# Attention in front of a mixture of experts: softmax scaling moved behind the product with v, float32 scores in batch 0

## The chip, the cores and the metric

One core of a Trainium2 chip. The metric is device time in microseconds of one launch. TensorE (PE) multiplies, VectorE (DVE), ScalarE (ACT) and GpSimd (POOL) do elementwise work, and SyncE (SP) issues most DMAs. A matmul takes a stationary operand, which a weight load (PEld) brings in, and streams a moving operand past it into PSUM; ScalarE and VectorE read PSUM, GpSimd works on SBUF only.

## The reference

Three stages in a row, float32 in and out:

1. Attention with 2 batches, 8 heads, 576 positions and 64 columns a head. The score of query i and key j is `q.k/8 - (cum[i] - cum[j])`, where `cum` is the running sum of `max(s, 0)`; keys behind the query are masked. The row is shifted by its maximum, `exp` is taken, and it is divided by its sum plus 1e-9. The result is multiplied with `v`.
2. A mixture of 8 experts over the 1152 tokens (512 wide, 1024 hidden): gates by `exp` of logits and eight rounds of row and column normalisation, then `relu(x @ w1) @ w2` of every expert, weighted and summed.
3. A feed-forward layer of 2048 hidden units with softplus.

## The kernel before, in words

Products are exact enough because each float32 operand is split in a rounded part and a rest (`h` and `l`, type F32R): a product of two split operands is three F32R matmuls, h*h, h*l and l*h. An unsplit F32 matmul is one call in the code; in the trace it is two TensorE instructions.

Attention works on pairs of heads, four pairs in each batch, eight in all (p = 0 to 7). The two heads lie in the two halves of the 128 partitions, so a score matmul uses 64 rows for each head and the two run side by side. A pair has five units (i = 0 to 4): units 0 to 3 are blocks of 128 queries, with 128, 256, 384 and 512 keys; unit 4 is the last 64 queries of both heads together (576 keys, stationary operand `ends`, 128 rows). For a unit the steps are:

- `scores`: q*k as products of split operands (unit 0: one F32 matmul), plus one F32R matmul that adds the bias from the running sums (`bq`, `bk`, `be`).
- `softmax` on VectorE (mask, minimum, negated), `expo` on ScalarE (exp and row sum), `norm`: VectorE takes the reciprocal of the row sum, GpSimd multiplies the unit's exponentials by it.
- `transp` on TensorE, `evac` on ScalarE (PSUM to SBUF), `attend` on TensorE: `v` times the transposed block, F32, one half of the array's columns for each head. Units 0 to 3 collect in one PSUM tile `pv`, unit 4 in `pv4`.
- After unit 3 and after unit 4, ScalarE (`do_X`) and VectorE (`do_Y`) split the result into `xh` and `xl`.

The order of work is written out by hand. A loop over n issues, in the order `YSUKAXVWBTPED`, `scores` of unit n+1 (S), `transp` of unit n-LT (T), `evac` of n-LV (V), `attend` of n-LA (A), `softmax` of n (B), `expo` of n (E), with LN, LT, LV, LA = 2, 3, 4, 5. K splits q and k of the next pair (hi on ScalarE, rest on GpSimd), D copies the last 64 queries into `ends`, W splits the first expert's weights, U (from n = `ready`) runs the first group of the first expert's up product between attention units. Each engine works through its own instructions in order. PSUM tiles rotate: `sc` has 4 buffers (two units), `tr` has 2, `pv` has 1.

At the start the running sums are split into four arrays (`cs`, each also negated), written to DRAM (`c8d`), and read back into single partitions of `bk`, `bq` and `be` (`load_bias`, L245 to L251). All of these DMAs, the loads of q, k, v and the raw weights are issued by SP in program order. After attention the experts and the last layer run as one long stream of matmuls (`up`, L127; `down`, L174).

Of the kernel before, what the change touches and what calls it, by code (L numbers as in the profile page):

```python
# [14 lines left out]
ALU = mybir.AluOpType  # L15
# [5 lines left out]
def attention_moe_ffn(ctx, tc, q, k, v, s, w_gate, w1, w2, w_in, w_out, out):  # L21
# [59 lines left out]
    def prep_steps(e, which, i, parts=1):  # L81

        if e >= NE:
            return
        key = (e, which, i)
        t = raw_t.pop(key)
        hi = w_p.tile([P, WQ], F32R, tag=f"w{which}h", name=f"w{which}h")
        lo = w_p.tile([P, WQ], F32R, tag=f"w{which}l", name=f"w{which}l")
        c = KD if which == 1 else TQ
        wt[key] = (hi.rearrange("p (c n) -> p c n", c=c), lo.rearrange("p (c n) -> p c n", c=c))  # L90
        nc.scalar.activation(out=hi, in_=t, func=AF.Copy)  # L91
        for a in range(parts):
            yield
            r = slice(a * WQ // parts, (a + 1) * WQ // parts)
            (nc.gpsimd if parts > 1 else nc.vector).tensor_tensor(out=lo[:, r], in0=t[:, r], in1=f(hi[:, r]),  # L95
                                                                  op=ALU.subtract)
        load_next()
# [92 lines left out]
    with tc.manual_schedule():  # L190
# [3 lines left out]
        with ExitStack() as att:  # L194
            early = ExitStack()
            eb_p = [(early.enter_context(tc.tile_pool(name="eb", bufs=10)), 10)]
# [23 lines left out]
            def load_rest(p):  # L220
                b, hp = divmod(p, NP)
                if p > 0:
                    load_bias(p)
# [13 lines left out]
            def init_bias(x):  # L237
                for t in (bq_t[x], bk_t[x], be_t[x]):
                    nc.gpsimd.memset(f(t), 0.0)
                for j in range(2):  # L240
                    for t, cols in ((bq_t[x], slice(0, S)), (bk_t[x], slice(0, S)),
                                    (be_t[x], slice(j * REM, (j + 1) * REM))):
                        nc.gpsimd.memset(f(t[j * D:j * D + 4, cols]), 1.0)  # L243

            def load_bias(p):  # L245
                for j in range(2):
                    h = 2 * p + j
                    nc.sync.dma_start(out=f(bk_t[p % BB][j * D + 2:j * D + 4, :]), in_=c8d[h, 0:2, :])
                    nc.sync.dma_start(out=f(bq_t[p % BB][j * D:j * D + 2, :]), in_=c8d[h, 2:4, :])
                    nc.sync.dma_start(out=f(be_t[p % BB][j * D:j * D + 2, j * REM:(j + 1) * REM]),  # L250
                                      in_=c8d[h, 2:4, NB * P:])  # L251
# [3 lines left out]
            for n in range(4):  # L255
                load(n)
# [8 lines left out]
            cs = [eb_tile(B * H, f"cs{x}").bitcast(F32R) for x in range(4)]  # L265
            c8d = dr.tile([B * H, 4, S], F32, name="c8d")
            for a, b in ((0, 2 * P), (2 * P, S)):
                x = c8[:, a:b]
                nc.scalar.activation(out=cs[0][:, a:b], in_=x, func=AF.Copy)
                nc.scalar.activation(out=cs[2][:, a:b], in_=x, func=AF.Copy, scale=-1.0)  # L270
                nc.vector.tensor_tensor(out=cs[1][:, a:b], in0=x, in1=f(cs[0][:, a:b]), op=ALU.subtract)
                nc.vector.tensor_tensor(out=cs[3][:, a:b], in0=f(cs[0][:, a:b]), in1=x, op=ALU.subtract)
            for x in range(4):
                nc.sync.dma_start(out=c8d[:, x, :], in_=f(cs[x]))
            load_bias(0)
            make_identity(nc, ident)
# [15 lines left out]
            for x in ends:  # L292
                for y in x:
                    nc.gpsimd.memset(f(y), 0.0)
# [3 lines left out]
            def split(n, engine=nc.gpsimd):  # L298

                p, r = divmod(n, 2)  # L300
                if p >= B * NP:
# [9 lines left out]
            def split_ends(p):  # L311
# [3 lines left out]
                t = pair[p]  # L315
                t["ends"] = ends[p % 2]
                for y, z in zip(ends[p % 2], (t["qh"], t["ql"])):
                    for j in range(2):
                        r = slice(j * D, (j + 1) * D)
                        o = y[r, j * REM:(j + 1) * REM]  # L320
                        if p > 0:
                            nc.sync.dma_start(out=f(o), in_=f(z[r, W:]))
                        else:
                            nc.vector.tensor_copy(o, f(z[r, W:]))
# [4 lines left out]
            def scores(u):  # L329
# [5 lines left out]
                if i > 0:  # L335
                    kh, kl = t["kh"], t["kl"]
                else:
                    for j, x in enumerate(sc):
                        r = slice(j * D, (j + 1) * D)
                        nc.tensor.matmul(x[:, :P], qk_t[2 * p + 1][r, :P], qk_t[2 * p][r, :P], start=True, stop=False)  # L340
                    for j, x in enumerate(sc):
                        r = slice(j * D, (j + 1) * D)
                        nc.tensor.matmul(x[:, :P], bq[r, :P], bk[r, :P], start=False, stop=True)
                    return
                if i < NB:
                    kp = (i + 1) * P
                    qs = slice(i * P, (i + 1) * P)
                    qh, ql = t["qh"], t["ql"]
                    for n, (a, b) in enumerate(((qh, kh), (qh, kl), (ql, kh), (bq, bk))):
                        for j, x in enumerate(sc):  # L350
                            r = slice(j * D, (j + 1) * D)
                            nc.tensor.matmul(x[:, :kp], a[r, qs], b[r, :kp], start=(n == 0), stop=(n == 3))  # L352
                else:
                    qh, ql = t["ends"]
                    for z, ks in ((sc[0][:, :S - 2 * P], slice(0, S - 2 * P)), (sc[1][:, :2 * P], slice(S - 2 * P, S))):
                        for n, (a, b) in enumerate(((qh, kh), (qh, kl), (ql, kh), (be, bk))):
                            nc.tensor.matmul(z, a, b[:, ks], start=(n == 0), stop=(n == 3))  # L357

            load_rest(0)
            scores(units[0])  # L360
            for n in range(2):
                split(n, nc.vector if n else nc.gpsimd)
            split_ends(0)
            load(4)
            load(5)
            load_next()
            load_next()

            def softmax(u, before):

                p, i = u
                l = live[u]
                st = ap2.tile([P, 8], F32, tag="st", name="st", bufs=6)
                l["st"], l["eb"] = st, []
                if i < NB:
                    kk = (i + 1) * P
                    for j, sc in enumerate(l["sc"]):
                        eb = eb_tile()
                        l["eb"].append(eb)
                        next(before, None)  # L380
                        nc.vector.tensor_tensor_reduce(eb[:, :kk], sc[:, :kk], mask[:, W - kk:], -0.125, BIG,  # L381
                                                       ALU.add, ALU.min, st[:, j:j + 1])
                else:
# [3 lines left out]
                    next(before, None)  # L387
                    nc.vector.tensor_tensor_reduce(eb[:, S - 2 * P:], y[:, :2 * P], mask4[:, S - 2 * P:], -0.125, BIG,
                                                   ALU.add, ALU.min, st[:, 4:5])
                    next(before, None)  # L390
                    nc.vector.tensor_tensor_reduce(eb[:, :S - 2 * P], x[:, :S - 2 * P], mask4[:, :S - 2 * P], -0.125, BIG,
                                                   ALU.add, ALU.min, st[:, 5:6])
                    nc.vector.tensor_tensor(st[:, 0:1], st[:, 4:5], st[:, 5:6], ALU.min)
                for _ in before:
                    pass

            def expo(u):
                p, i = u
                l = live[u]
                st = l["st"]  # L400
                kk = (i + 1) * P if i < NB else S
                for j, eb in enumerate(l["eb"]):
                    nc.scalar.activation(out=eb[:, :kk], in_=eb[:, :kk], func=AF.Exp, bias=st[:, j:j + 1],  # L403
                                         scale=-1.0, accum_out=st[:, 2 + j:3 + j])

            def norm(u):
                p, i = u
                l = live[u]
                st = l["st"]
                m = 2 if i < NB else 1  # L410
                kk = (i + 1) * P if i < NB else S
                nc.vector.tensor_scalar(st[:, 2:2 + m], st[:, 2:2 + m], 1e-9, None, ALU.add)
                yield
                nc.vector.reciprocal(st[:, 6:6 + m], st[:, 2:2 + m])
                for j, eb in enumerate(l["eb"]):
                    nc.gpsimd.tensor_scalar(eb[:, :kk], eb[:, :kk], st[:, 6 + j:7 + j], 1.0, ALU.mult, ALU.mult)
# [29 lines left out]
            def evac(u):  # L446
                for o, x in live[u].pop("ev"):
                    nc.scalar.activation(out=o, in_=x, func=AF.Copy)

            def attend(u):  # L450
                p, i = u
                t, pt = pair[p], live.pop(u)["pt"]
                b, hp = divmod(p, NP)
                vv = t["vv"]
                if i == 0:
                    t["pv"] = ps.tile([P, 512], F32, tag="y1", name="pv", bufs=1)
                if i < NB:
# [6 lines left out]
                    pv, cols = t["pv"], slice(b * S, b * S + NB * P)  # L464
                else:
                    pv = ps.tile([P, 512], F32, tag="tr", name="pv4", bufs=2)[:, :REM]
                    for c in range(NB + 1):
                        r, x = (P, pt[:, 0, c, :]) if c < NB else (REM, pt[:REM, 1, 0, :])
                        for j in range(2):
                            nc.tensor.matmul(pv[j * D:(j + 1) * D, :], vv[:r, c, j, :], x[:, j * REM:(j + 1) * REM],  # L470
                                             start=(c == 0), stop=(c == NB), skip_group_check=True)
                    cols = slice(b * S + NB * P, (b + 1) * S)
                    pair.pop(p)
                done.append((pv, xh[:, hp, cols], xl[:, hp, cols]))

            done = []

# [21 lines left out]
            LN, LT, LV, LA, LX, LY = 2, 3, 4, 5, 1, 1  # L499
# [6 lines left out]
            def do_S(n):  # L506
                if unit(n + 1):
                    p, i = unit(n + 1)
                    scores((p, i))
                    if i == 0:  # L510
                        load(2 * p + 4)
                        load(2 * p + 5)
# [15 lines left out]
            def do_X(n):  # L528
                for pv, h_, l_ in xs.get(n - LX, ()):
                    nc.scalar.activation(out=h_, in_=pv, func=AF.Copy)  # L530

            def do_Y(n):
                for pv, h_, l_ in xs.get(n - LX - LY, ()):
                    nc.vector.tensor_tensor(out=l_, in0=pv, in1=f(h_), op=ALU.subtract)

            def do_B(n):
                before = iter(norm(unit(n - LN)) if unit(n - LN) else ())
                if unit(n):
                    softmax(unit(n), before)
                for _ in before:  # L540
                    pass
# [31 lines left out]
            for n in range(nu + LA + LX + LY + 1):  # L573
                if n == half:
                    eb_p.append((ap2, 8))
# [7 lines left out]
                if n < nu:  # L583
                    p, i = units[n]
                    if i == 1 and p + 1 < B * NP:
                        load_rest(p + 1)
# [238 lines left out]
```

## Time and profile before

| | |
|---|---|
| median of 3 runs | 1125.5 us (1125.14 to 1125.92) |
| profiled execution | 1125.42 us, span of the trace 1123.6 us |
| PE busy | 1107.6 us (99%) |
| DVE, ACT, POOL busy | 585.9, 393.1, 197.1 us (52%, 35%, 18%) |
| attention | from the start to about 123 us |

In the rows, an instruction's "us" or "ns" is its latency; matmuls overlap, so what one costs in a dense stream is the distance from its start to the next start. "<-" inside brackets names what ended an engine's idle time before it.

### The profile page before, as it was taken

Reading aid. Unit: us, or ns where it says so; the run is one execution under the profiler, and the core shown is the slowest. Engines: PE = TensorE matmul, PEld = TensorE weight load, DVE = VectorE, ACT = ScalarE, POOL = GpSimd, SP = SyncE. Lnnn points to the kernel's source line nnn. Section 1 sums busy time; section 2 is a strip of 40 time slices with the busy share of each in tenths; the row PEclk is TensorE's granted clock in tenths of the full one; section 3 lists DMA queues with packets and bytes.
Section 4 is the critical chain, followed back from the end, with each engine's and each line's share of the span. In section 5 each row is a group of like instructions: output and inputs, shape, how many; then the busy total and the mean of one; then the engine's idle time right before and its main releaser. Section 6 shows DMA issues by size and latency. Waiting matters only on the chain.

```text
span 1123.6 us, 15723 instructions
## 1 busy us (share of the span) xinstructions
PE 1107.6 (99%) x6104; PEld 987.7 (88%) x6104; DVE 585.9 (52%) x1189; ACT 393.1 (35%) x775; POOL 197.1 (18%) x252
## 2 busy tenths in 40 slices
PE   5999999999999999999999999999999999999998
PEld 4777889999999999999999989999999999999997
DVE  6654227264654546465446545544532367566663
ACT  6987312222221222123122212222221246565541
POOL 8875000000101010110101010101100022222220
PEclk9999999999999999999999999999999999999999
DMA  4331201121331223233122221413220112010001
GB/s 155 108 121 35 95 1 38 38 103 48 113 104 57 66 94 104 75 99 117 51 72 94 103 76 66 131 47 113 76 76 1 38 38 76 1 57 19 20 19 47
DMA packets 30346, 78.37 MB, mean 70 GB/s; under 512 B 5936, under 2 KB 10544, under 8 KB 30272
## 3 DMA queue, kind: packets, MB, share of 16 engines
q1 hardware_dynamic: 27712, 68.98, 18.7%
q0 software_dynamic: 2560, 8.39, 1.9%
q8 instruction: 48, 0.79, 0.3%
q14 instruction: 26, 0.21, 0.1%
HBM read 66.01 MB, written 10.90 MB: 68 GB/s over the span
## 4 chain that ended last, share of the span: by engine, by line
PE 98%; POOL 1%; ACT 0%; issue 0%; DVE 0%; POOLq 0%; ACTq 0%
PE ph L127 45%; PE py L174 44%; PE pv L460 2%; PE sc L352 2%; PE tr L434 1%; PE tr L428 1%; PE sc L357 1%; PE pv L470 1%; PE tr L440 0%; PE pg L620 0%; PE px L707 0%; PE sc L340 0%; POOL bk L243 0%; POOL bq L243 0%; ACT eb L403 0%
## 5 line engine op out<-in xcount | busy, mean ns | idle before, releaser
L127 PE MATMUL ph<-xh,w1h 128*128 128x384 f32 x960 | 325.1, 339 | 0.0
L127 PE MATMUL ph<-xl,w1h 128*128 128x384 f32 x960 | 322.4, 336 | 0.0
L127 PE MATMUL ph<-xh,w1l 128*128 128x384 f32 x960 | 322.3, 336 | 0.0
L174 PE MATMUL py<-w2h,hl 128*128 128x512 f32 x720 | 284.3, 395 | 0.0
L174 PE MATMUL py<-w2l,hh 128*128 128x512 f32 x720 | 283.6, 394 | 0.0
L133 DVE SCALAR_TENSOR_TENSOR hl<-ph,hh 128x384 fp32r<-128x384 f32 x192 | 106.8, 557 | 332.1 <-ACT hh L132 332.0
L174 PE MATMUL py<-w2h,hh 128*128 128x512 f32 x720 | 279.8, 389 | 0.0
L132 ACT ACTIVATE hh<-ph 128x384 fp32r<-128x384 f32 x192 | 94.5, 492 | 495.4 <-PE ph L127 495.3
L127 PEld LDWEIGHTS ph<-xh,w1h 128*128 128x128 f32 x960 | 180.3, 188 | 10.2 <-issue 0.7
L127 PEld LDWEIGHTS ph<-xl,w1h 128*128 128x128 f32 x960 | 180.3, 188 | 8.9
L127 PEld LDWEIGHTS ph<-xh,w1l 128*128 128x128 f32 x960 | 180.2, 188 | 0.0
L174 PEld LDWEIGHTS py<-w2h,hl 128*128 128x128 f32 x720 | 135.0, 188 | 28.6
L174 PEld LDWEIGHTS py<-w2l,hh 128*128 128x128 f32 x720 | 135.0, 187 | 22.5
L174 PEld LDWEIGHTS py<-w2h,hh 128*128 128x128 f32 x720 | 135.3, 188 | 22.0
L697 POOL TENSOR_TENSOR cm<-cm,ct 128x512 f32<-128x512 f32 x32 | 42.8, 1339 | 620.8 <-DVE ct L696 620.8
L147 POOL TENSOR_TENSOR a<-a,a 128x384 f32<-128x384 f32 x48 | 48.9, 1018 | 247.7 <-DVE a L145 247.7
L95 DVE TENSOR_TENSOR w2l<-raw,w2h 128x1024 fp32r<-128x1024 f32 x38 | 46.4, 1222 | 30.7 <-ACT w2h L91 30.7
L180 DVE SCALAR_TENSOR_TENSOR acc<-py,gate,acc 128x512 f32<-128x512 f32 x63 | 47.2, 750 | 19.7 <-PE py L174 19.6
L95 DVE TENSOR_TENSOR w1l<-raw,w1h 128x1024 fp32r<-128x1024 f32 x36 | 46.4, 1290 | 12.8 <-ACT w1h L91 12.2
L91 ACT ACTIVATE w2h<-raw 128x1024 fp32r<-128x1024 f32 x40 | 42.2, 1057 | 24.2 <-PE py L174 18.7
L151 ACT ACTIVATE hh<-a 128x384 fp32r<-128x384 f32 x48 | 25.3, 527 | 71.2 <-DVE a L150 71.2
L403 ACT ACTIVATE eb<-eb,st 128x128 f32<-128x128 f32 (+4 forms) x72 | 41.6, 584 | 7.2 <-DVE st L381 6.8
(150 smaller groups left out, 939.0 us busy)
## 6 DMA issues: line engine op xcount, KB each, us to landing
raw<-in_w SPq DMA_DIRECT2D x64, 512.0 KB
f<-in_w_in SPq DMA_DIRECT2D x16, 512.0 KB
f<-in_w_out SPq DMA_DIRECT2D x16, 512.0 KB
wd<-cm POOLq DMA_DIRECT2D x32, 256.0 KB, 4.7
raw<-wd SPq DMA_DIRECT2D x16, 512.0 KB
qk<-in_k SPq DMA_DIRECT2D x8, 288.0 KB
qk<-in_q SPq DMA_DIRECT2D x8, 288.0 KB
out<-o SPq DMA_DIRECT2D x9, 256.0 KB
```

The lines of the kernel that those rows point to most:

```text
L91: nc.scalar.activation(out=hi, in_=t, func=AF.Copy)
L95: (nc.gpsimd if parts > 1 else nc.vector).tensor_tensor(out=lo[:, r], in0=t[:, r], in1=f(hi[:, r]), op=ALU.subtract)
L127: nc.tensor.matmul(ph, a, b, start=(n == 0), stop=(n == len(ops) - 1))
L132: nc.scalar.activation(out=hh, in_=ph, func=AF.Relu)
L133: nc.vector.scalar_tensor_tensor(out=hl, in0=ph, scalar=0.0, in1=f(hh), op0=ALU.max, op1=ALU.subtract)
L147: nc.gpsimd.tensor_tensor(out=a2, in0=a1, in1=a2, op=ALU.subtract)
L151: nc.scalar.activation(out=hh, in_=a3, func=AF.Copy)
L174: nc.tensor.matmul(py, x, y, start=(ft == 0 and n == 0), stop=(ft == NFT - 1 and n == 2))
L180: nc.vector.scalar_tensor_tensor(out=a, in0=py, scalar=gate_t[0][:, tt, e:e + 1], in1=a, op0=ALU.mult, op1=ALU.add)
L352: nc.tensor.matmul(x[:, :kp], a[r, qs], b[r, :kp], start=(n == 0), stop=(n == 3))
L403: nc.scalar.activation(out=eb[:, :kk], in_=eb[:, :kk], func=AF.Exp, bias=st[:, j:j + 1], scale=-1.0, accum_out=st[:, 2 + j:3 + j])
L697: nc.gpsimd.tensor_tensor(out=m, in0=m, in1=f(t), op=ALU.add)
```

## The change

- `norm` no longer scales the exponentials. The nine row sums of a pair are kept in `sm`; after unit 3 and after unit 4 VectorE takes their reciprocals (`rc`). In `attend`, after unit 3, eight F32 matmuls spread the reciprocals over the rows of a PSUM tile `rb` (stationary: a column of `rc`, broadcast to 64; moving: `ident`, 128 columns); after unit 4 one transpose does the same for `pv4`. `do_X` copies that to SBUF (`rs`, ScalarE) and multiplies the product with v by it (VectorE) into `xf`. `do_Y` splits `xf` into `xh` and `xl`, on GpSimd for pairs 0 to 6 and on ScalarE and VectorE for pair 7. The GpSimd stage being gone, LN, LT, LV, LA become 1, 2, 3, 4.
- In batch 0 (p < 4) the scores are one F32 matmul instead of three F32R ones; q and k are not split there, and `ends` becomes a float32 tile `endf` loaded from DRAM.
- `evac`: the second tile of units 2 and 3 and both tiles of unit 4 go to VectorE.
- The first expert's early weight pieces are rounded and subtracted on GpSimd (before: rounded on ScalarE in one instruction).
- The bias has two arrays instead of four (the sign moves into the constant rows). Pair 0 takes them from SBUF (`cs`) instead of DRAM; the write to DRAM follows. v of pair 0 is loaded ahead of q and k of pair 1; q and k are loaded one pair ahead instead of two.

```diff
-        nc.scalar.activation(out=hi, in_=t, func=AF.Copy)
-        for a in range(parts):
+        if parts == 1:
+            nc.scalar.activation(out=hi, in_=t, func=AF.Copy)
             yield
...
+        else:
+            for a in range(parts):
+                yield
+                r = slice(a * WQ // parts, (a + 1) * WQ // parts)
+                nc.gpsimd.tensor_copy(hi[:, r], t[:, r])
+                nc.gpsimd.tensor_tensor(out=lo[:, r], in0=t[:, r], in1=f(hi[:, r]), op=ALU.subtract)
...
+                    x = c8d[h] if p > 0 else f(cs[h:h + 1])
+                    for t, r, cols in ((bk_t, 2, slice(0, S)), (bq_t, 0, slice(0, S))):
+                        nc.sync.dma_start(out=f(t[p % BB][j * D + r:j * D + r + 2, :]), in_=x)
...
+                if p < NP or i == 0:
+                    kf, qf = qk_t[2 * p], qk_t[2 * p + 1]
+                    prod = [(t["ends"][0] if i == NB else qf, kf)]
+                else:
                     kh, kl = t["kh"], t["kl"]
+                    qh, ql = t["ends"] if i == NB else (t["qh"], t["ql"])
+                    prod = [(qh, kh), (qh, kl), (ql, kh)]
+                prod.append((be if i == NB else bq, bk))
...
-                for j, eb in enumerate(l["eb"]):
-                    nc.gpsimd.tensor_scalar(eb[:, :kk], eb[:, :kk], st[:, 6 + j:7 + j], 1.0, ALU.mult, ALU.mult)
+                if i < NB - 1:
+                    return
+                c = slice(0, 2 * NB) if i < NB else slice(2 * NB, 2 * NB + 1)
+                sm, rc = pair[p]["sm"], pair[p]["rc"]
+                nc.vector.tensor_scalar(rc[:, c], sm[:, c], 1e-9, None, ALU.add)
+                nc.vector.reciprocal(rc[:, c], rc[:, c])
...
+                for n, (o, x) in enumerate(live[u].pop("ev")):
+                    if i == NB or n == 1:
+                        nc.vector.tensor_copy(o, x)
+                    else:
+                        nc.scalar.activation(out=o, in_=x, func=AF.Copy)
...
+                    rb = ps.tile([P, 512], F32, tag="tr", name="rb", bufs=2)
+                    for c in range(NB):
+                        for j in range(2):
+                            nc.tensor.matmul(rb[j * D:(j + 1) * D, c * P:(c + 1) * P],
+                                             rc[:, 2 * c + j:2 * c + j + 1].to_broadcast([P, D]), ident,
+                                             start=True, stop=True, skip_group_check=True)
...
+                    nc.tensor.transpose(pv[:, P:2 * P], rc[:, 2 * NB:].to_broadcast([P, P]), ident)
...
-            LN, LT, LV, LA, LX, LY = 2, 3, 4, 5, 1, 1
+            LN, LT, LV, LA, LX, LY = 1, 2, 3, 4, 1, 1
...
+                for rs, rb, ops in xs.get(n - LX, ()):
+                    nc.scalar.activation(out=rs, in_=rb, func=AF.Copy)
+                    for o, pv, r in ops:
+                        nc.vector.tensor_tensor(out=o, in0=pv, in1=r, op=ALU.mult)
```

## Rows read from the trace of the kernel before

**Rows 1.** The page: engines' busy time, and the chain that ended last.
```profile
PE 1107.6 (99%) x6104; PEld 987.7 (88%) x6104; DVE 585.9 (52%) x1189; ACT 393.1 (35%) x775; POOL 197.1 (18%) x252
...
PE 98%; POOL 1%; ACT 0%; issue 0%; DVE 0%; POOLq 0%; ACTq 0%
```

**Rows 2.** Busy us (and count) by engine in two stretches: pair 1, pair 5.
```profile
core 0: us, PE busy (x) PEld busy (x) DVE busy (x) ACT busy (x) POOL busy (x), PEclk, DMA share, GB/s
30.49:41.87 11.38, 11.38 (x125) 8.85 (x124) 7.06 (x34) 11.13 (x32) 10.32 (x16) 1.00 0.45 133
...
77.53:93.73 16.20, 16.20 (x148) 12.79 (x147) 7.35 (x35) 11.40 (x33) 7.67 (x11) 1.00 0.09 25
```

**Rows 3.** Waits of PE, 13 to 75 us: total us, times, longest.
```profile
PE sc L352 <- POOL kl L309: 2.0, 1, 2.0
PE tr L434 <- ACT pt L448: 0.2, 1, 0.2
```

**Rows 4.** Timeline of PE at the start: start us, latency us, count last.
```profile
5.01 0.80 PE L340 MATMUL sc<-qk 64*128 64x128 f32 x4 [5.01 <-DMA qk<-in_q]
...
11.02 0.44 PE L343 MATMUL sc<-bk,bq 64*128 64x128 f32 x1 [0.40 <-DMA bq<-c8d]
11.03 0.76 PE L352 MATMUL sc<-kh,qh 64*128 64x256 f32 x2
13.79 0.58 PE L352 MATMUL sc<-kl,qh 64*128 64x256 f32 x2 [2.00 <-POOL kl L309]
...
14.59 0.53 PE L352 MATMUL sc<-kh,qh 64*128 64x384 f32 x2
14.91 0.53 PE L352 MATMUL sc<-kl,qh 64*128 64x384 f32 x2
...
18.88 0.68 PE L428 MATMUL tr<-ident,eb 128*128 128x128 f32 x2
19.49 0.71 PE L340 MATMUL sc<-qk 64*128 64x128 f32 x3
```

**Rows 5.** Timeline of SP's queue and of VectorE at the start.
```profile
5.46 1.89 SPq L274 DMA_DIRECT2D c8d<-cs  x4
...
9.55 0.25 SPq L249 DMA_DIRECT2D bq<-c8d  x1
...
5.60 0.47 DVE L271 TENSOR_TENSOR cs<-c,cs 16x320 fp32r<-16x320 f32 x1
```

**Rows 6.** Timeline of PE in pairs 2 and 3, some rows.
```profile
44.03 0.28 PE L352 MATMUL sc<-kl,qh 64*128 64x256 f32 x2
44.15 0.28 PE L352 MATMUL sc<-kh,ql 64*128 64x256 f32 x2
...
48.94 0.39 PE L352 MATMUL sc<-kh,ql 64*128 64x512 f32 x2
49.17 0.39 PE L352 MATMUL sc<-bk,bq 64*128 64x512 f32 x2
49.49 0.88 PE L460 MATMUL pv<-pt,vv 128*64 128x128 f32 x12
50.30 0.66 PE L440 MATMUL tr<-ident,eb 128*128 128x128 f32 x4
...
52.06 1.09 PE L460 MATMUL pv<-pt,vv 128*64 128x128 f32 x16
53.09 0.44 PE L428 MATMUL tr<-ident,eb 128*128 128x128 f32 x2
53.45 0.49 PE L340 MATMUL sc<-qk 64*128 64x128 f32 x4
```

**Rows 7.** Instruction groups by shape, 0 to 290 us: count, busy us, mean ns.
```profile
L448 ACT ACTIVATE pt<-tr 128x512 f32<-128x512 f32 x32 | 18.2, 596 | 4.2 <-PE tr L440 2.0 <-PE tr L428 1.5 <-PE tr L434 0.7
L534 DVE TENSOR_TENSOR xl<-pv,xh 128x512 fp32r<-128x512 f32 x8 | 5.5, 685 | 0.9 <-ACT xh L530 0.8
```

**Rows 8.** GpSimd's scaling line, 0 to 125 us: count, min/median/max ns.
```profile
L416 POOL TENSOR_SCALAR eb<-eb,st x72: 365/584/756, 18.5 to 114.8; 128x128 f32<-128x128 f32 x16, 128x256 f32<-128x256 f32 x16, 128x384 f32<-128x384 f32 x16, 128x512 f32<-128x512 f32 x16
```

More of the change, by code (lines that the diff above doesn't have):

```diff
@@ L291, in attention_moe_ffn @@
             ends = [[ac.tile([P, P], F32R, name=f"end{x}{y}") for y in "hl"] for x in range(2)]
[L292 to L294 removed]
+            endf = [eb_p[0][0].tile([P, P], F32, tag=f"endf{x}", name=f"endf{x}", bufs=1) for x in range(2)]
+            for y in endf + ends[0] + ends[1]:
+                nc.gpsimd.memset(f(y), 0.0)
             for x in range(1, BB):
@@ L347, in scores, with softmax @@
                     qs = slice(i * P, (i + 1) * P)
-                    qh, ql = t["qh"], t["ql"]
-                    for n, (a, b) in enumerate(((qh, kh), (qh, kl), (ql, kh), (bq, bk))):
+                    for n, (a, b) in enumerate(prod):
                         for j, x in enumerate(sc):
                             r = slice(j * D, (j + 1) * D)
-                            nc.tensor.matmul(x[:, :kp], a[r, qs], b[r, :kp], start=(n == 0), stop=(n == 3))
+                            nc.tensor.matmul(x[:, :kp], a[r, qs], b[r, :kp], start=(n == 0), stop=(n == m))
                 else:
-                    qh, ql = t["ends"]
                     for z, ks in ((sc[0][:, :S - 2 * P], slice(0, S - 2 * P)), (sc[1][:, :2 * P], slice(S - 2 * P, S))):
[L356 to L362, printed above, removed]
+                        for n, (a, b) in enumerate(prod):
+                            nc.tensor.matmul(z, a, b[:, ks], start=(n == 0), stop=(n == m))
             split_ends(0)
-            load(4)
-            load(5)
             load_next()
             load_next()
-            def softmax(u, before):
+            scores(units[0])
+            def softmax(u):
                 p, i = u
                 l = live[u]
-                st = ap2.tile([P, 8], F32, tag="st", name="st", bufs=6)
+                st = ap2.tile([P, 4], F32, tag="st", name="st", bufs=6)
                 l["st"], l["eb"] = st, []
@@ L393, in softmax @@
-                    nc.vector.tensor_tensor(st[:, 0:1], st[:, 4:5], st[:, 5:6], ALU.min)
-                for _ in before:
-                    pass
+                                                   ALU.add, ALU.min, st[:, 3:4])
+                    nc.vector.tensor_tensor(st[:, 0:1], st[:, 2:3], st[:, 3:4], ALU.min)
             def expo(u):
                 p, i = u
-                l = live[u]
-                st = l["st"]
+                l, t = live[u], pair[p]
+                if i == 0:
+                    t["sm"] = ap2.tile([P, 2 * NB + 1], F32, tag="sm", name="sm", bufs=2)
+                    t["rc"] = ap2.tile([P, 2 * NB + 1], F32, tag="rc", name="rc", bufs=2)
```

139 lines of the change are left out of this document (61 added, 78 removed).

## Prediction

> **What bounds the kernel now.** I read the page's busy times and its chain first. TensorE is busy 99% of the span and makes up 98% of the chain that ended last [rows 1]; no other engine has more than 1% of the chain. A busy matmul row is a latency, though, and rows overlap, so I looked next at whether TensorE is really the pace in the stretch that the change touches. Pairs 1 and 5 take 11.38 and 16.20 us, with TensorE covering both in full [rows 2]. ScalarE, at 11.13 of 11.38 us in pair 1, could pace TensorE just as well; in pair 5 it has 11.40 of 16.20 us, and the pieces of TensorE's work in the timeline have the same lengths there. So TensorE's own work is the pace. The view of waits says the same: from 13 to 75 us its matmuls wait 2.0 us for GpSimd's first split and 0.2 us for an eviction [rows 3]. Last the start: TensorE does four matmuls at 5.01 us, gets the last bias of unit 0 at 11.02, then stands until the split of k at 13.79, and works densely from there [rows 4].
>
> From this follows how each edit is priced: work added to TensorE in attention costs its full length, work taken off ScalarE or GpSimd after about 14 us is worth nothing, and what starts TensorE earlier is worth its full length. The sum is made against the profiled execution, 1125.42 us (span 1123.6 and 1.8 around it), which stands 0.1 under the median of 1125.5.
>
> **The start.** Pair 0 no longer needs a split, so what TensorE waits for is the bias. Before, the subtraction that closes the second chunk starts at 5.60 us and takes 0.47, four DMAs go to DRAM from 5.46 on, and the last bq read is issued at 9.55 and used at 11.02, 1.47 us later [rows 4, 5]. Now two arrays are ready at about 6.0, and four DMAs out of SBUF at 0.3 us each put the last one at 6.9 us in the queue. With 1.5 us to land and 0.3 because v of pair 0 is now ahead of it in the transfers, that is 8.7 us. It can't be earlier than 8.0; with no gain at all it is 11.0. From 8.7 on TensorE has units 1, 2 and 3 in front of it; the VectorE work that frees `sc` buffers (unit 0's two reductions) lies beside unit 1's scores. Dense work starting at 8.7 in place of 13.79: -5.1 us. One product of unit 1, done at 11.03 before [rows 4], now lies behind the start: +0.2. The filling before had its own holes: two transposes with what follows took 0.61 us at 18.88 against 0.36 at 53.09 [rows 4, 6], about 1 us over the first unit after it; with GpSimd out of that chain I take half of it: -0.5. At 14.59 two products of 384 columns start 0.32 us apart, which is 1.2 GHz, against 0.23 for 512 later, which is 2.4 [rows 4, 6]; the engine had stood idle before. I expect the same slow first microseconds after the new start, so no difference, give or take 0.8.
>
> **Float32 scores in batch 0.** No F32 matmul wider than 128 columns is in the trace. The nearest is v times the transposed block: three key blocks take 50.30 - 49.49 = 0.81 us, four take 53.09 - 52.06 = 1.03, so one block of 128 columns, with its two passes for each head and the heads side by side, is 0.22 us [rows 6]. An F32R product of 256 columns is 0.12 and of 512 columns 0.23. Scaling the 0.22 with columns, the F32 product of units 1, 2, 3 costs 0.44, 0.66, 0.88 against three F32R ones at 0.36, 0.52, 0.69; unit 4, 576 columns in all, 0.99 against about 0.81. That is +0.08, +0.14, +0.19, +0.18, or +0.58 a pair and +2.3 us for four pairs. The upper end is this; the lower end takes a wide pass to be as fast as an F32R one, two passes for three: -0.12 - 0.17 - 0.23 - 0.27 = -0.8 a pair, -3.2 in all. I take the upper one, since it is read from the same kind of instruction.
>
> [...]
>
> **Scaling behind the product.** After unit 3 TensorE gets eight F32 matmuls, four blocks of 128 columns for two heads: the shape of one key block each, 4 x 0.22 = 0.88 us a pair, 7.0 us for eight. It lies on the path, since TensorE has no idle time there; nothing hides it. If a broadcast stationary operand were free to load it would still stream, so I see no lower end much under 0.8; the upper is 1.2, should the array drain between it and v's product. After unit 4 one transpose: between 0.11 (a 128-column pass) and 0.18 (half of the 0.36 for two at 53.09), +0.9 us for eight pairs.
>
> **What costs nothing while TensorE is the pace.** GpSimd loses 9 scalings a pair, 0.58 us at the median [rows 8], and gets the early roundings and two instructions of `do_Y`: less work in sum. ScalarE loses four evictions a pair (0.6 us for 512 columns) and in batch 0 the splits, and gets one copy of `rb` and one of 128 columns. VectorE gets these four evictions, at the 0.60 of ScalarE's eviction or the 0.69 of its own subtraction from PSUM [rows 7], about 2.3 us, and the products with `rs` in place of the subtractions: at most 7.1 + 2.3 = 9.4 of a pair's 12.9 us, where it had 7.1 of 11.4. The cover of all this is TensorE's unit, a fifth of 11.38 us or more; the rival B is what happens without it. Reads of q and k one pair ahead are issued by SP two units before ScalarE splits them; I take 0.5 us for waits of this kind in sum, and take as much off for waits of before, so these cancel.
>
> [...]
>
> **Sum.** -5.1 + 0.2 - 0.5 + 2.3 + 7.0 + 0.9 = +4.8 us, from 1125.4 to 1130.2. Its own range: the start 0.7 better or 1.5 worse, scores 0.5 lower, the slow first stretch 0.8 either way: 1128 to 1133.
>
> **Rivals.** A: wide F32 passes stream like F32R. Then -3.2 stands in place of +2.3 and the time is 1124.7, not slower than before. It decides from a pass of 512 columns at 0.23 us instead of 0.44. For it: the narrow blocks may be bound by loading the stationary operand, not by streaming. Against it: two passes of 128 columns take four times an F32R share.
>
> B: VectorE holds TensorE up. In the unit where `rb` is copied, its product waits for ScalarE's copy (its forerunner waited 0.9 us in all eight pairs together [rows 7]), takes 0.69, and only then come the two reductions of the next unit, which free the `sc` buffers for the scores after. I put the slack there at a few tenths of a microsecond; half a microsecond lost a pair is 4 us: 1134.2. For it: four evictions a pair now stand in VectorE's queue as well. Against it: the same order stood before with a subtraction of the same size, and TensorE waited 0.2 us in all.
>
> C: the bias comes no earlier, because its small transfers queue behind the loads of v too, and land as late as before. Then TensorE starts at 11.0 and the time is 1132.5. Against it: the DRAM round trip is gone in any case.
>
> **Chances.** My forecast 0.60, A 0.14, B 0.13, C 0.07, something unnamed that makes it faster 0.06. A change of 0.2% (2.3 us) is about what a measurement of this kernel tells from none. Slower holds B, C and most of my forecast (0.55 of its 0.60): 0.75. Within: the low end of the forecast and most of A: 0.14. Faster: the rest, 0.11. The range that leaves about 2 in 10 outside takes A's value and B's in: 1124.5 to 1134.5.
>
> **What would show it.** In the trace after: TensorE's dense work from about 8.7 us on; eight matmuls for `rb` taking 0.9 us behind each unit 3; score groups of 384 and 512 columns in batch 0 0.14 and 0.19 us longer than now; a pair in batch 0 of about 12.9 us in place of 11.38, one in batch 1 of 17.2 in place of 16.20; from the experts on the same trace, shifted. I am wrong if the F32 groups are shorter than the split ones, if pairs grow by more than 1.8 us, or if TensorE starts later than 10 us.

## The result, and the profile after

The changed kernel takes 1138.9 us (median of four runs, 1137.6 to 1139.3) where the kernel before takes 1125.5: 1.0117 times as long, 95% interval 1.0099 to 1.0134. The forecast was 1130.2 with a range to 1134.5; the direction was right, the size was not. Against the profiled execution of before, 1125.4, the profiled execution after is 1139.0, a loss of 13.6 us.

The page of the kernel after, busy times and the chain that ended last, against [rows 1]:

```profile
PE 1119.1 (98%) x6208; PEld 994.0 (87%) x6208; DVE 597.9 (53%) x1175; ACT 372.4 (33%) x728; POOL 170.9 (15%) x209
...
PE 96%; DVE 2%; ACT 1%; POOL 1%; DMA 1%; issue 0%; SPq 0%; POOLq 0%; DVEq 0%
```

TensorE is 11.5 us busier, so most of the loss looks like added matmuls. But VectorE, ScalarE, GpSimd and a DMA now stand in the chain with 5% together, where they had 1%: TensorE also waits. The stretches of one pair each show where (windows of the kernel after from one unit 0 to the next, pairs 1 to 5, against pairs 1 and 5 of [rows 2]):

```profile
30.39:44.50 14.11, 13.21 (x134) 9.40 (x133) 9.07 (x32) 7.86 (x25) 6.36 (x10) 1.00 0.35 105
44.50:59.23 14.73, 13.40 (x134) 9.43 (x133) 9.07 (x32) 8.97 (x27) 8.80 (x12) 1.00 0.36 101
59.23:73.85 14.62, 12.87 (x142) 9.88 (x141) 9.17 (x32) 8.79 (x27) 8.28 (x11) 1.00 0.33 103
73.85:90.32 16.47, 15.19 (x154) 11.84 (x153) 9.64 (x33) 9.69 (x28) 6.27 (x7) 1.00 0.29 93
90.32:107.48 17.16, 17.16 (x166) 13.73 (x165) 10.19 (x34) 9.99 (x29) 4.94 (x4) 1.00 0.20 58
```

The second column is the length, the third TensorE's busy time. Here as in [rows 2], a stretch goes by the pair whose products with v fill it; the scores in it are those of the next pair, so of these five only the first two (scores of pairs 2 and 3) hold F32 ones. Pair 5, in batch 1, is covered by TensorE in full and takes 17.16 us for 16.20: +0.96, the price of the added matmuls alone. Pairs 1 to 4 have 0.9 to 1.8 us each in which TensorE does nothing. Pair 1 takes 2.73 us more than before, of which 0.97 are the reciprocals and 0.47 the F32 scores (below); the remaining 1.3 are waits. The same subtraction, from the kernel before cut at the same matmul, gives about 1.7, 2.0 and 1.8 for pairs 2 to 4, with 0.4 at the tail 7.2 us in all. Pair 5 has none: there, matmuls of the first expert stand between attention units.

What the matmuls themselves cost, from TensorE's timeline of the kernel after in pair 1 (start, latency, what; groups of one kind are one row, so read the distance between starts):

```profile
38.14 1.13 PE L352 MATMUL sc<-qk 64*128 64x512 f32 x4
...
39.43 1.09 PE L452 MATMUL pv<-pt,vv 128*64 128x128 f32 x16
40.35 1.04 PE L459 MATMUL rb<-ident,rc 128*64 128x128 f32 x16
41.33 0.44 PE L416 MATMUL tr<-ident,eb 128*128 128x128 f32 x2
```

The F32 scores of unit 3 take 39.43 - 38.14 = 1.29 us, against 1.12 for the split ones before (26.53 - 25.41, in the kernel before):

```profile
25.41 0.50 PE L352 MATMUL sc<-kh,qh 64*128 64x512 f32 x2
...
26.53 0.33 PE L460 MATMUL pv<-pt,vv 128*64 128x128 f32 x2
```

The spreading of the reciprocals takes 41.33 - 40.35 = 0.98, of which 0.10 is the switch that v's product had at its end before (40.35 - 39.43 = 0.92 for 1.03): net 0.87.

What TensorE waits for, 30 to 91 us of the kernel after (total us, times, longest):

```profile
PE tr L422 <- DVE pt L438: 3.0, 4, 0.8
PE tr L422 <- ACT pt L440: 1.2, 4, 0.5
PE tr L431 <- ACT pt L440: 1.1, 2, 0.7
```

**The first wait** is on VectorE. Its timeline and GpSimd's in pair 1 of the kernel after:

```profile
32.38 1.32 DVE L383 TENSOR_TENSOR st<-st 128x1 f32<-128x1 f32 x1
33.62 0.16 DVE L403 TENSOR_SCALAR rc<-sm 128x8 f32<-128x8 f32 x1
33.81 0.20 DVE L404 RECIPROCAL rc<-rc 128x8 f32<-128x8 f32 x1
33.93 0.51 DVE L438 COPY pt<-tr 128x384 f32<-128x384 f32 x1
```
```profile
31.53 0.66 POOL L545 CAST xh<-xf 128x576 fp32r<-128x576 f32 x1 [11.42 <-DVE xf L536]
32.27 1.40 POOL L546 TENSOR_TENSOR xl<-xf,xh 128x576 fp32r<-128x576 f32 x1
```

A minimum of two single columns takes 1.32 us, and it ends (33.70) with the subtraction that `do_Y` now does on GpSimd (33.67). Behind it in VectorE's queue is the eviction of a transposed tile (L438), which ends at 34.44; TensorE's next transposes (L422), which need a `tr` buffer, begin at 34.49.

**The second wait** is on ScalarE: its split of k waits for the load. The waits of ScalarE, then of SP, for 30 to 91 us of the kernel after:

```profile
ACT kh L312 <- DMA qk<-in_k: 4.3, 3, 1.7
```
```profile
SPq L228 <- PE pv L472: 38.6, 5, 8.7
```

SP's loads of v wait for the buffer that the last v product of an earlier pair frees, and the loads of q and k, now issued only one pair ahead, stand behind them in the same queue. The chain that ended last runs through one such case:

```profile
43.88 0.27 PE pv L472
...
46.71 4.68 DMA qk<-in_k
...
52.01 0.59 ACT pt L440
...
52.64 0.30 PE tr L431
```

What ScalarE does after the split, evictions among it, comes later by that much. Only q and k of batch 1 are split, and the first split, for pair 4, falls in pair 2's stretch, so this wait can't stand in pair 1.

**The start.** SP's timeline and TensorE's in the kernel after, against [rows 4, 5]:

```profile
6.05 0.73 SPq L252 DMA_DIRECT2D bk<-cs  x1
6.83 0.57 SPq L252 DMA_DIRECT2D bq<-cs  x1
7.51 0.56 SPq L252 DMA_DIRECT2D bk<-cs  x1
8.11 0.56 SPq L252 DMA_DIRECT2D bq<-cs  x1
```
```profile
9.92 0.44 PE L352 MATMUL sc<-bk,bq 64*128 64x128 f32 x1 [0.79 <-DMA bq<-cs]
...
12.75 1.91 PE L352 MATMUL sc<-qk 64*128 64x512 f32 x3
...
15.20 0.69 PE L416 MATMUL tr<-ident,eb 128*128 128x128 f32 x2
...
17.97 0.33 PE L452 MATMUL pv<-pt,vv 128*64 128x128 f32 x2
```

Dense work begins at 9.92 us. The scores of unit 3 take 15.20 - 12.75 = 2.45, against the 1.29 of the same group in pair 1: about half the pace. The granted clock of the window, third from the end, reads 1.00:

```profile
12.00:14.00 2.00, 2.00 (x11) 1.53 (x8) 1.18 (x6) 1.36 (x5) 0.00 (x0) 1.00 0.57 172
```

But the trace has no record of the granted clock before 15.77 us (kernel before: 17.12), and the view shows 1.00 where it has none. So the slow stretch goes from 9.92 to about 15.8 us here and from 13.79 to about 17.1 before.

At 17.97 TensorE has done what it had done at 20.89 before:

```profile
20.89 0.39 PE L352 MATMUL sc<-kh,qh 64*128 64x256 f32 x2
```

That is the whole gain of the start, 2.9 us, with pair 0's F32 scores in it.

### The profile page after: what moved, and what is told of

The parts are those of the page before. It is cut to its first block, busy times and chain, and to the rows that moved or that the text cites. A ratio compares the mean times of both kernels' runs of the same rounds, so it can differ in the third digit from the quotient of the medians.

```text
span 1137.1 us, 15634 instructions
## 1 busy us (share of the span) xinstructions
PE 1119.1 (98%) x6208; PEld 994.0 (87%) x6208; DVE 597.9 (53%) x1175; ACT 372.4 (33%) x728; POOL 170.9 (15%) x209
## 4 chain that ended last, share of the span: by engine, by line
PE 96%; DVE 2%; ACT 1%; POOL 1%; DMA 1%; issue 0%; SPq 0%; POOLq 0%; DVEq 0%
PE ph L131 44%; PE py L178 44%; PE sc L352 2%; PE pv L452 1%; PE tr L422 1%; PE rb L459 1%; PE sc L356 0%; DVE st L383 0%; ACT eb L393 0%; DMA qk<-in_k 0%; PE pg L635 0%; PE tr L428 0%; PE px L722 0%; DVE xf L536 0%; PE pv L470 0%
## 5 line engine op out<-in xcount | busy, mean ns | idle before, releaser
L393 ACT ACTIVATE eb<-eb,st 128x128 f32<-128x128 f32 (+4 forms) x72 | 41.5, 578 | 35.8 <-DVE st L373 19.6
L94 DVE TENSOR_TENSOR w1l<-raw,w1h 128x1024 fp32r<-128x1024 f32 x36 | 46.4, 1289 | 12.8 <-ACT w1h L92 11.8
```

Source lines behind the costliest of these rows:

```text
L94: nc.vector.tensor_tensor(out=lo, in0=t, in1=f(hi), op=ALU.subtract)
```

## The experiments

Times are medians, the kernel before at 1125.5 to 1125.9 in each comparison, the changed kernel 1138.9.

**The waits, one at a time.** First theory: GpSimd's subtraction holds VectorE. Rival: VectorE has too much to do, whatever GpSimd does.

e1_min_reduce:

```diff
-                    nc.vector.tensor_tensor(st[:, 0:1], st[:, 2:3], st[:, 3:4], ALU.min)
+                    nc.vector.tensor_reduce(st[:, 0:1], st[:, 2:4], AX.X, ALU.min)
```

> Kernel after, with unit 4's minimum of two row minima taken by a reduction over two neighbouring columns (one operand) instead of an elementwise operation on two. Theory 1: that elementwise minimum takes 1.32 us because GpSimd's subtraction of do_Y runs at the same time, and the exponentials and evictions behind it are late. Then it falls below 0.4 us and the time to 1133 to 1136, unless the next VectorE operation with two SBUF accesses (adding 1e-9 to the row sums) is held up instead, which would leave 1136 to 1138. Theory 2: VectorE simply has too much work in the units without expert work beside them (evictions and multiplications); the minimum gets shorter, the waits stay, 1138 to 1139.

Measured: 1137.6 (ratio 1.0105, 1.0088 to 1.0121), 1.3 us less. VectorE's groups of that kernel from 25 to 137 us:

```profile
L403 DVE TENSOR_SCALAR rc<-sm 128x8 f32<-128x8 f32 x7 | 8.9, 1268 | 0.0
...
L383 DVE TENSOR_REDUCE st<-st 128x1 f32<-128x2 f32 x7 | 1.1, 155 | 0.2
```

The minimum is quick (155 ns for 1325), and the next instruction, the addition of 1e-9, takes 1268 in its place. So ScalarE gets the minimum in time, but the eviction is about as late as before (TensorE waits 2.7 us for it instead of 3.0). The stall isn't the minimum's own: in pair 1 of e1 the addition starts at 32.19 and ends at 33.45, and GpSimd's subtraction ends at 33.42.

e2_y_act_dve moves `do_Y` of all pairs to ScalarE and VectorE:

```diff
-                    if p + 1 < B * NP:
+                    if False:
```

> Kernel after, with do_Y on ScalarE (copy) and VectorE (subtraction) for all pairs, so GpSimd's subtraction is gone and VectorE has 0.76 us a pair more. Theory 1 (GpSimd's subtraction holds VectorE up): the minimum falls from 1.32 to 0.2 us, the pairs 1 to 4 lose most of their 7 us of waits, 1132 to 1136. Theory 2 (too much work on VectorE): slower than after, 1140 to 1143.

Measured: 1139.4 (1.0124, 1.0109 to 1.0139), no gain. VectorE's groups there:

```profile
L403 DVE TENSOR_SCALAR rc<-sm 128x8 f32<-128x8 f32 x7 | 1.2, 165 | 0.0
L383 DVE TENSOR_TENSOR st<-st 128x1 f32<-128x1 f32 x7 | 1.1, 159 | 0.2
```

Both instructions are at 0.16 us again: GpSimd's subtraction was what stretched them, that much is shown. But its work now lies on ScalarE and VectorE, and while TensorE's waits for VectorE's evictions fall from 3.0 to 0.9 us, those for ScalarE's grow from 2.3 to 5.1. As an account of all of the lost time, the theory fell.

e3_evac_act puts all evictions back on ScalarE:

```diff
-                for n, (o, x) in enumerate(live[u].pop("ev")):
-                    if i == NB or n == 1:
-                        nc.vector.tensor_copy(o, x)
-                    else:
-                        nc.scalar.activation(out=o, in_=x, func=AF.Copy)
+                for o, x in live[u].pop("ev"):
+                    nc.scalar.activation(out=o, in_=x, func=AF.Copy)
```

> Kernel after, with all evictions on ScalarE as before. Theory 1: the evictions no longer queue behind the held up minimum, the exponentials of unit 4 still do: 1135 to 1138. Theory 2 (VectorE's work, of which the evictions are the new part): nearly all waits go, 1131 to 1134. A third theory, that the pipeline shortened by one unit is what makes each delay visible, expects no change or ScalarE's queue in VectorE's place, 1138 to 1141.

Measured: 1140.4 (1.0132, 1.0117 to 1.0147). The rival's 1131 to 1134 fell, but the run doesn't decide alone: TensorE now waits 7.6 us for ScalarE's evictions, so a gain on VectorE could be hidden by the load on ScalarE. The third theory, the shorter pipeline, has its time; e5 below bears on both.

e4_min_norm is e1 with the addition gone as well (the 1e-9 is left out of the sum):

```diff
-                nc.vector.tensor_scalar(rc[:, c], sm[:, c], 1e-9, None, ALU.add)
-                nc.vector.reciprocal(rc[:, c], rc[:, c])
+                nc.vector.reciprocal(rc[:, c], sm[:, c])
```

> As e1_min_reduce, and the addition of 1e-9 to the row sums is left out (the sums are 1 or more), so that neither VectorE operation is left that was seen to stretch beside GpSimd's subtraction. Theory 1: 1132 to 1135, and clearly under e1 if there the addition took over the wait. Theory 2: as e1, 1138.

Measured: 1137.1 (1.0104, 1.0089 to 1.0119). No instruction of VectorE is stretched any more, and still only 1.8 us come back. The waits of TensorE and of ScalarE there, 30 to 91 us:

```profile
PE tr L430 <- ACT pt L439: 3.1, 3, 1.5
...
ACT kh L312 <- DMA qk<-in_k: 7.0, 3, 2.9
```

ScalarE reaches the split of k sooner, and waits 7.0 us for the load instead of 4.3. The gain was given back to a wait that had stood behind the first one.

e5_both adds to e4 that the splits are issued a unit later, which gives the load a unit more; e6_late has only this edit, on the changed kernel:

```diff
-                    if 1 <= i <= 2:
-                        m = 2 * (p + 1) + i - 1
+                    if 2 <= i <= 3:
+                        m = 2 * (p + 1) + i - 2
```

> The changed kernel with VectorE's minimum of unit 4 taken over one operand, the 1e-9 left out of the reciprocal (both as in the run before), and in addition the splits of q and k of the next pair issued one unit later, so that their load has a unit more to land. Theory: two waits lie behind one another, the minimum beside GpSimd's subtraction and ScalarE's split that waits for the late load and holds its evictions back; only with both gone does TensorE stop waiting. Then about 4 us under the 1137.1 of the kernel with the first one gone, 1132 to 1134, and no transpose in pairs 1 to 4 takes over 1 us. Rival: the pipeline, one stage shorter, leaves too little slack between softmax and transpose whatever the loads do; then 1136 to 1138, and the transposes of unit 4 still wait, for another engine.

> The changed kernel with only the splits of the next pair one unit later. Theory (two waits behind one another): the minimum still ends with GpSimd's subtraction, so little is gained, 1137 to 1139. Rival (the late load alone is what TensorE waits for): the same gain as with both edits, 1132 to 1134.

Measured: e5 1133.1 (1.0065, 1.0050 to 1.0080), e6 1137.4 (1.0103, 1.0088 to 1.0118). Alone the edits are worth 1.8 and 1.5 us, together 5.8. Both times lie where the theory had them. The pairs of e5, in windows like those above:

```profile
29.89:43.13 13.24, 13.04 (x133) 9.41 (x132) 7.66 (x30) 7.97 (x25) 6.36 (x10) 1.00 0.41 112
43.13:56.45 13.32, 13.05 (x134) 9.42 (x133) 7.66 (x30) 9.20 (x27) 8.13 (x11) 1.00 0.38 112
56.45:69.21 12.76, 12.49 (x141) 9.86 (x140) 7.66 (x30) 8.80 (x27) 7.54 (x10) 1.00 0.38 118
69.21:84.57 15.36, 14.84 (x153) 11.80 (x152) 8.21 (x31) 9.88 (x29) 7.61 (x9) 1.00 0.33 100
84.57:101.73 17.16, 17.16 (x165) 13.73 (x165) 8.84 (x32) 10.05 (x29) 4.95 (x4) 1.00 0.20 58
```

Pairs 1 to 4 are 0.9, 1.4, 1.9 and 1.1 us shorter than in the changed kernel, pair 5 is the same to the hundredth. In pair 1, where nothing is split, e4 alone already gains the whole 0.9 (13.23 us). In pairs 2 to 4 e4 gains 0.8 in sum (14.97, 14.04, 15.97), e6 1.6 (14.18, 13.72, 16.32), both 4.4. That settles most of the waits: there are two, and where both stand, either one hides a good part of the other. The evictions and products that VectorE got are all still there in e5, and from 30 to 91 us no wait of TensorE for VectorE is left: VectorE's load as such is not the cause. Nor is the shorter pipeline by itself the cause of these 5.8 us, though whether the one unit more of before would have covered both waits was not tried.

**The added matmuls.** e9_rb_twice is e5 with the spreading issued twice:

```diff
-                    for c in range(NB):
+                    for c in [*range(NB)] * 2:
                         for j in range(2):
                             nc.tensor.matmul(rb[j * D:(j + 1) * D, c * P:(c + 1) * P],
```

> The kernel with both waits mended (1133.1), with the eight F32 matmuls that spread the reciprocals issued twice into the same place, eight more a pair; the result is the same. Theory: they lie on the path at their full length, 0.87 us a pair in the trace of the changed kernel, 7.0 for eight: 1140.1. Rival: part of their length only fills a wait that would be there anyway (for v's products, or for the next scores); then less than 4 us more, under 1137.

Measured: 1140.0 (1.0132, 1.0117 to 1.0147), 6.9 more than e5. Each pair is 0.8 to 0.9 us longer than in e5: nothing hides these matmuls.

**The start.** e7_warm is the changed kernel with

```diff
+            hot = ps.tile([P, 512], F32, tag="y2", name="hot", bufs=1)
+            for _ in range(24):
+                nc.tensor.matmul(hot[:, :P], ones, ones, start=True, stop=True)
             scores(units[0])
```

> The changed kernel with 24 F32 matmuls of 128 columns, on constants, into a PSUM tile of their own ahead of the first scores; their results are not used. They keep TensorE busy from about 3 us until the first bias lands, at 9.9. Theory: the 6 us after 9.9 in which products come at 1.2 GHz spacing follow from TensorE having stood idle; with it busy they come at 2.4 GHz spacing sooner, and 2 to 3 us are saved: 1136 to 1137. Rival: the slow stretch belongs to the time since the launch or to these products; then 1138 to 1139.5.

Measured: 1136.9 (1.0098, 1.0083 to 1.0114). TensorE there:

```profile
11.44 1.02 PE L352 MATMUL sc<-qk 64*128 64x512 f32 x3
...
12.90 0.44 PE L419 MATMUL tr<-ident,eb 128*128 128x128 f32 x2
```

The scores of unit 3 take 1.46 us at most instead of 2.45, and the record of the granted clock begins with 1.00 at 6.39 us (15.77 in the changed kernel), so here the slow pace goes with an engine that had stood idle, not with these products. But the time is right by luck. Of the 2.3 us gained by the transposes of unit 0, 0.6 are left when the scores of pair 2 begin (29.82 for 30.39 us), after a wait of 1.1 for the bias of pair 1. The other 1.6 come later, where k is split: those pairs take 14.26, 13.73 and 16.23 us, close to e6's, and ScalarE waits 2.0 us for k there instead of 4.3. Why the loads land sooner here was not taken apart.

The slow stretch also differs between executions of the same start: in e2 to e5 the record begins with 1.00 at 12.8 to 13.8 us, in e1, e6 and e9 at 15.1 to 15.9. By the scores of pair 2 that, too, is worth 0.7 us or less (29.73 to 30.39 us; e9 left out).

b1_start turns to the kernel before and gives it the start alone (two bias arrays, pair 0's from SBUF, v of pair 0 earlier, F32 scores without splits for pair 0; two buffers fewer for the exponentials):

```diff
+                    x = c8d[h] if p > 0 else f(cs[h:h + 1])
+                    for t, r, cols in ((bk_t, 2, slice(0, S)), (bq_t, 0, slice(0, S))):
+                        nc.sync.dma_start(out=f(t[p % BB][j * D + r:j * D + r + 2, :]), in_=x)
...
+                if p == 0 or i == 0:
+                    kf, qf = qk_t[2 * p], qk_t[2 * p + 1]
+                    prod = [(t["ends"][0] if i == NB else qf, kf)]
```

> The kernel before with only the start of the change: two bias arrays, pair 0's bias read from SBUF, v of pair 0 loaded ahead of q and k of pair 1, F32 scores and no splits for pair 0 alone, and two fewer buffers for the exponentials, which the room needs. The scaling stays where it was, on GpSimd. The start was worth 2.9 us in the changed kernel; without the rest of the change 1122 to 1123.5 is expected if the start is a gain of its own. Rival: with the scaling on GpSimd in the way of the early units, or fewer buffers, the start gives nothing back: 1125 to 1126.

Measured: 1123.6 (0.9979, 0.9970 to 0.9989): the start is a gain of 2.2 us, and this version beats both kernels, if by little.

Three runs tried to add the unused matmuls to it. b2_warm has them and the bias of pair 1 ahead of the raw weights, b4_warm_only the matmuls alone, b5_warm_later is b2 with the first expert's weight pieces begun two units later:

```diff
+            load_bias(1)
             load_next()
             load_next()
...
-                if n >= 3:
+                if n >= 5:
                     next(prework, None)
```

> The kernel before with the start of the change (1123.6), 24 F32 matmuls on constants ahead of the first scores, unused, that keep TensorE busy until the first bias lands, and the bias of pair 1 read ahead of the first raw weights. Theory: the products of the first 4 us come at 2.4 GHz spacing, 2.9 us earlier, and the wait for the bias of pair 1 (1.1 us in the changed kernel with the same matmuls) is gone: 1120.7 to 1121.6. Rival: what comes earlier runs into the loads of v and of the raw weights, and is given back: 1122.5 to 1123.6.

> The kernel before with the start of the change (1123.6) and the 24 unused matmuls ahead of the first scores, the order of the loads left as it is. Theory: the products of the first 4 us come at 2.4 GHz spacing, and what stood between (1127.4) was ScalarE waiting for the raw weights that had been put behind the bias, 2.6 us of idle TensorE, and the lower clock after that; without it 1120.5 to 1122.5, with a wait of about 1 us for the bias of pair 1 left. Rival: an earlier start is taken back by any late load of pairs 0 and 1; then 1123 to 1125.

> The kernel before with the start of the change, the unused matmuls, the bias of pair 1 ahead of the raw weights (all as in the run at 1127.4), and the first expert's weight pieces begun two units later, so that ScalarE doesn't wait for them. Theory: neither wait is left, 1120 to 1121.5. Rival: the later weight pieces crowd into batch 1 or hold up the experts; then 1123 or more.

Measured: b2 1127.4 (1.0015, 1.0006 to 1.0025), b4 1123.9 (0.9990, 0.9980 to 1.0000), b5 1125.0 (0.9994, 0.9985 to 1.0003). All three missed. b4 and b5 lie where their rivals had them, b2 3.8 us above its rival's range. In b2 ScalarE waits for the raw weights, and the exponentials stand behind that (its wait, then windows with the granted clock in the third column from the end):

```profile
ACT w1h L91 <- DMA raw<-in_w: 3.0, 1, 3.0
```
```profile
18.00:20.00 2.00, 0.00 (x0) 0.00 (x0) 0.00 (x0) 2.00 (x5) 1.19 (x2) 1.00 1.06 340
20.00:22.00 2.00, 1.54 (x8) 1.03 (x9) 1.60 (x10) 2.00 (x9) 2.00 (x4) 0.52 0.87 241
22.00:24.00 2.00, 2.00 (x11) 1.40 (x10) 0.58 (x3) 2.00 (x7) 1.62 (x3) 0.50 0.54 202
```

TensorE stands still for 2 us and more, and is then granted about 0.50 until about 27 us. In b4 and b5 the earlier start runs into waits of 1.6 and 2.6 us between 9.9 and 24 us, for the bias, `endf`, evictions, reductions and the scaled exponentials.

**F32 scores without the scaling.** b3_f32 is b1 with F32 scores in all of batch 0; b3b_f32_loads issues its q and k loads later:

```diff
-                if p == 0 or i == 0:
+                if p < NP or i == 0:
...
-                    if i == (NB if p == 0 else 0):
+                    if i == (NB if p < NP else 0):
                         load(2 * p + 4)
                         load(2 * p + 5)
```

(the second edit in b3b alone)

> The kernel before with the start of the change (1123.6), and F32 scores without splits in the whole of batch 0 instead of pair 0 alone. Theory: the F32 groups of pairs 1 to 3 cost their difference in the trace of the changed kernel, 0.47 us a pair, 1.4 in sum: 1125.0. Rival: the splits taken off ScalarE and GpSimd give as much back: 1123.6 or less.

> As the last F32 kernel (the kernel before with the start of the change and F32 scores in all of batch 0; 1130.4), but in batch 0 the loads of q and k two pairs ahead are issued at unit 4 instead of unit 0, since unsplit q and k hold their buffers until unit 4's scores. Theory: the 6.7 us that kernel lost against 1123.6 were 5.3 of waiting behind a blocked SP queue (its TensorE waits 3.6 us for later pairs' biases) and 1.4 of F32 passes; with the queue free, 1125.0. Rival: the F32 passes themselves cost more than 0.47 us a pair; then 1127 or more.

Measured: 1130.4 (1.0063, 1.0039 to 1.0088; two of its six runs took 1136.3 and 1136.9) and 1130.2 (1.0040, 1.0025 to 1.0055), both missed. In b3 the loads wait 12.3 and 7.2 us in SP's queue for score matmuls that still read their buffers, and TensorE 3.6 us for a bias behind them. In b3b that is gone, and ScalarE waits again for k (waits of 40 to 64 us; then TensorE's timeline behind the second wait):

```profile
ACT kh L312 <- DMA qk<-in_k: 4.6, 2, 3.1
```
```profile
62.38 1.06 PE L426 MATMUL tr<-ident,eb 128*128 128x128 f32 x8 [2.39 <-ACT pt L440]
...
64.98 1.55 PE L452 MATMUL pv<-pt,vv 128*64 128x128 f32 x12
66.46 1.03 PE L432 MATMUL tr<-ident,eb 128*128 128x128 f32 x4
```

After 2.39 us of standing, v's product takes 1.48 us where it takes 0.81 elsewhere, at a granted clock of 0.50. The F32 groups have their lengths of the changed kernel, so the passes cost what they did there; what b3b adds to b1 is 1.4 for them, 4.1 of waits for ScalarE's evictions and the slow microseconds behind. F32 scores alone, with loads in time, were not measured.

## Why the prediction was wrong

- **"What costs nothing while TensorE is the pace" failed.** Two costs set at zero were 7.2 us together by the trace, and 5.8 by e5. One of the prediction's signs of being wrong came true: cut at the same matmul, pairs 1 to 4 grew by 2.7 to 3.1 us, more than the 1.8 that it allowed. First, the prediction gave VectorE's instructions fixed lengths and asked only whether their sum fits a unit; a 128x1 minimum of 0.16 us became 1.32 because of what GpSimd was doing. VectorE's rows of before already had the same minimum (L393) at 0.16 to 0.49 us and the same addition (L412) at 0.14 to 1.36. The two longest additions end with a subtraction of GpSimd (L309): one runs from 17.13 to 18.49 us, the subtraction from 17.04 to 18.47; the other from 71.66 to 72.99, the subtraction from 71.55 to 72.98. The later traces are alike: in pair 1 the minimum of the kernel after (1.32 us) began at 32.38 and the addition of e1 (1.26) at 32.19, 0.11 and 0.18 us behind GpSimd's subtraction, and both ended 0.03 behind its end, while e1's reduction, begun 0.10 behind it, took its 0.15; e2 has both at 0.16 without the subtraction. These two additions spoke against moving a 1.40 us subtraction to GpSimd in front of the minimum, and were not weighed.
- **The reads of q and k were priced at 0.5 us and cancelled.** What was counted was the time from issue to split; what counts is where the load stands in SP's queue, behind v's load, which waits up to 8.7 us for a buffer. I had not followed that queue. Nor did the prediction price the pipeline that became one unit shorter.
- **The start was forecast 1.9 us too good**: -5.4, or -4.8 with pair 0's F32 scores, against -2.9. The DMAs out of SBUF take 0.56 to 0.73 us each in the queue, not 0.3, so dense work begins at 9.92 instead of 8.7, 1.2 of the 1.9. The rest is the slow first stretch, which lasts some 6 us instead of 3.4; it is within the 0.8 set aside for it, and e7 has 0.6 of it back by the scores of pair 2. The prediction's 1.2 GHz is the pace of 384 columns in 0.32 us, its 2.4 an estimate, twice that; 512 columns in 0.23 us make 2.2 columns a ns. In b3b a score product of 512 columns takes 0.42 us (64.00 to 64.42) at a granted clock of 0.50, which is 1.2 again.
- **Right were the terms read from rows of the same kind.** `rb`: 0.87 a pair for 0.88, and 6.9 for 7.0 by e9. Transposes: 0.10 for 0.11. F32 scores: 0.08, 0.12, 0.175 and about 0.1 us for units 1 to 4, 0.47 a pair for 0.58. VectorE's eviction of 512 columns: 0.69, the upper of its two prices.
- **The rivals.** A fell: wide F32 passes cost more than split products (1.29 us for 1.12 in unit 3). B named VectorE and the right order of loss (1134.2), and half of the path: ScalarE's copy to `rs`, the product (0.69 us) and the next reductions stand in the chain that ended last, ahead of the stretched minimum. But TensorE waited for transposes' buffers, not for scores' `sc` buffers, and in e5, where the same products still wait for ScalarE, TensorE doesn't wait for VectorE. What B lacked is GpSimd. C fell: the bias came 1.1 us earlier than 11.02.

The sum as the runs have it: start -2.9, F32 scores of pairs 1 to 3 1.4, spreading and transposes 7.8, waits 7.2: +13.5, for 13.6 measured. Of the waits, 1.4 are still in e5, where the trace shows four waits of transposes for ScalarE's evictions, 1.3 us together, as the changed kernel has them (1.2); what makes those late was not taken apart, and loading q and k two pairs ahead in the changed kernel was not tried.

## What to carry to other kernels

When work moves to another engine, price what runs beside it as well as what it displaces: here a moved subtraction of 1.40 us stretched a minimum on VectorE from 0.16 us to 1.32, and the eviction queued behind it was late. Follow each moved load through its whole queue to the buffer it waits for. And when mending one wait returns little, look which engine now arrives early at the next one before giving the theory up.

## Not expected of the hardware

- A DMA of 4.5 KB out of one SBUF partition holds SP for 0.56 to 0.73 us; the same bias from DRAM takes 0.22 to 0.29.
- VectorE's reciprocal of eight columns (0.19 us in e4, 0.20 in the kernel after) and its copy from PSUM (0.51 for 384 columns in both) kept their lengths beside the same GpSimd subtraction: in e4 they began at 31.78 and 31.89 us, and it ran from 31.61 to 33.02.
- A TensorE that had stood for 2.4 us (b3b) and 2.6 us (b2) in the middle of attention came back and was soon granted 0.50, for 3 us in b3b and 7 in b2, so that these waits cost more than their length (in b3b v's product took 1.48 us for 0.81). At the start the slow pace (2.45 us for 1.29) shows in the distances between matmuls alone, since the granted clock isn't on record there.
